# Attention and two expert layers: weight conversion through ScalarE's rectifier, and fixed steps for weight maxima and gating sums

## Chip, cores and metric

One core of one Trainium2 chip runs the whole program. The metric is the device time of one execution in microseconds (us). A difference of 0.2% (about 4 us) is what a measurement of this kernel can tell from no change.

## What is computed

Three stages follow each other. Inputs are float32 except the three weight matrices of the second stage, which come as float64 (a float32 array times a float64 scalar).

```python
def _attn_ref(q, k, v, tau):                 # 4 x 8 heads, 576 x 64
    scores = scale * np.matmul(q, k.transpose(0, 1, 3, 2))
    thresh = np.max(scores, axis=-1, keepdims=True) - tau
    scores = np.where(scores >= thresh, scores, -1000000000.0)
    attn = softmax(scores)
    return np.matmul(attn, v)

def _moe_ref(x, w_gate, w_val, w_out, rms_g):    # 2304 tokens, 512 -> 1536 -> 512
    xn = x / rms * rms_g
    g = xn @ w_gate
    silu = g * (1.0 / (1.0 + np.exp(-g)))
    return (silu * (xn @ w_val)) @ w_out

def _moe2_ref(x, w_gate, w1, w2):            # 8 experts, 512 -> 1024 -> 512
    P = np.exp(x @ w_gate - max)
    for _ in range(8):
        P /= P.sum(1, keepdims=True) + 1e-09
        P /= P.sum(0, keepdims=True) + 1e-09
        P *= N / E
    for e in range(E):
        out += P[:, e:e + 1] * (np.maximum(x @ w1[e], 0.0) @ w2[e])
    return out
```

## The kernel before

Every float32 operand of a matmul is split into two float16 parts, and a product takes three matmuls.

**Attention** (`att_tile`, from line 283). A tile is 128 rows of one head. TensorE computes the scores `S` (line 294, two PSUM buffers), VectorE takes their maximum (308), ScalarE the exponential (312), VectorE keeps what is within `tau` of the maximum (314), ScalarE and GpSimd split the result into `hl` (319 to 321), SyncE transposes it by DMA into `eT`, and four tiles later TensorE multiplies with the values (351). Eight tiles, one for each head, make 128 tokens `x`; `finish_x` (from line 363) normalises them (VectorE's last operation is line 374) and SyncE transposes them into `xnT`.

**Second stage.** Two such blocks make 256 tokens, for which `mlp_in` (from line 544) multiplies with the gate and value weights (`gv`, line 551, twelve pairs of PSUM tiles) and `mlp_out` (from line 573) with the output weights (585). Before the first of these the float64 weights must be converted. `prep_group` takes the gate weights (`wgate`) and value weights (`wval`) in 24 loads of 128 rows of 512 numbers; `prep_out` takes the output weights (`wo`) in 12. Each load is two 32-bit words for a number, read by `words` (434; four buffers for the 24 loads, two for the 12), and `to_f32` (445) makes float32 of it: the high word, read as a float32 and scaled by 2^-112, has the right bits but for a shift by three; ScalarE scales it (453), VectorE takes three bits from the low word (454), shifts and joins (456), and puts the sign bit back from the high word (457). ScalarE then squares the result for the scale (477 or 511), and each load is scaled and split: ScalarE 486 and VectorE 487 for gate and value; VectorE 528, ScalarE 529 and GpSimd 530 for the output weights. The first `mlp_in` needs gate and value weights, the first `mlp_out` the output weights. A planner sets the order of the instructions on each engine from priorities; attention has the higher one, and weight pieces fill in where it expects an engine to be free.

**Third stage** (its loop from line 1177). Its order on TensorE is written by hand. `ahead` is a list of steps `k`; a step is six matmuls of the first product (`X` or `Z`, line 1051), and after it come one or two pieces of six matmuls of the second product (`P`, line 1119). Fourteen steps make a round: three blocks of 128 pairs of tokens with seven pieces each, 21 pieces. The second products use three PSUM banks; the piece `j == 1` alone opens the bank with the tag `mx`, and VectorE empties it (1129 or 1133). Besides the logits at the stage's start, the same bank serves two things: the maximum of a half expert's weights over the partitions (`all_max`, 136, through `over_partitions`: TensorE 131, VectorE 133), and in the gating the maximum of the logits (`lgtop`) and the eight column sums (`cs`, line 1000, read by VectorE 1002). So a `P` of piece 1 that follows one of these waits until VectorE has read it, and one of these that follows a `P` of piece 1 waits until VectorE has emptied that.

The preparation of a half expert's weights (`weight`, from 787) is a generator of 17 pieces, and `AT` (831) lists the steps, counted from a base, at which they are issued; piece five is the maximum, pieces six to nine are GpSimd's four sums (823). For the first matrix of an expert the base is a multiple of 14, for the second it is 7 more.

```python
    AT = (0, 4, 6, 8, 10, 10, 11, 13, 15, 12, 14, 16, 17, 19, 21, 23, 24)
            for n in due.pop(k, ()):
                with behind():
                    next(n, None)
```

`sinkhorn` (974) is the gating: a generator, started at step 36 and advanced by one piece a step, six pieces an iteration, so that the column sums come at steps 43, 49, ... 85. Its result `lg` is needed by `coefs` (1014), by ScalarE's scaling of the accumulators (1158), and by VectorE's first accumulation with a coefficient (1129).

Of the kernel before, what the change touches and what calls it, by code (L numbers as in the profile page):

```python
# [7 lines left out]
F32 = mybir.dt.float32  # L8
# [3 lines left out]
AF = mybir.ActivationFunctionType  # L12
ALU = mybir.AluOpType
# [6 lines left out]
def kernel(  # L20
# [24 lines left out]
    V, A, G, T = nc.vector, nc.scalar, nc.gpsimd, nc.tensor  # L45
    B, H, S, D = q.shape
    NT, DM = out.shape
    DFF = moe_w_gate.shape[1]
    E, _, FF = moe2_w1.shape
# [11 lines left out]
    def small(shape, name, dt=F32, bufs=1):  # L61
        return p0.tile(shape, dt, tag=name, name=name, bufs=bufs)
# [65 lines left out]
    def over_partitions(col, eye, name):  # L128

        ps = psm.tile([P, P], F32, tag="mx", name=name + "p", bufs=1)  # L130
        T.matmul(ps, lhsT=col.to_broadcast([P, P]), rhs=eye, start=True, stop=True)
        m = small([P, 1], name, bufs=2)
        V.tensor_reduce(m, ps, AX.X, ALU.max)  # L133
        return m
# [310 lines left out]
    def to_f32(dst, word, name):  # L445

        lw = pw.tile([P, 2, 2, HD], F16, tag="xs", name=name, bufs=2)
        lw = lw.rearrange("p o l n -> p (o l n)").bitcast(I32)
        A.activation(dst, word[:, :, 1].bitcast(F32), AF.Copy, scale=2.0**-112)
        V.tensor_scalar(lw, word[:, :, 0], 29, None, ALU.logical_shift_right)
        di = dst.bitcast(I32)
        V.scalar_tensor_tensor(lw, di, 3, lw, ALU.logical_shift_left, ALU.bitwise_or)
        V.scalar_tensor_tensor(
            di, word[:, :, 1], -(2**31), lw, ALU.bitwise_and, ALU.bitwise_or
        )
        return lw  # L460

    staged = [0]
# [297 lines left out]
    @contextmanager  # L760
    def behind():

        with ExitStack() as es:
            for ins in main.values():
                es.enter_context(tc.issue_after(ins.ins))
            yield
# [61 lines left out]
            yield  # L828
        (w1, w2)[which - 1][h], (inv1, inv2)[which - 1][h] = w, inv

    AT = (0, 4, 6, 8, 10, 10, 11, 13, 15, 12, 14, 16, 17, 19, 21, 23, 24)

    w1, w2, inv1, inv2 = {}, {}, {}, {}

    def w_pool(h):
        return pb if h % 2 == 0 else pc
# [137 lines left out]
    def sinkhorn():  # L974

        V.scalar_tensor_tensor(
            lg, lg, ginv[:, 0:1], inv_tok.to_broadcast([P, NTL, E]), ALU.mult, ALU.mult
        )
        mx = small([P, 1], "lgm")
        V.tensor_reduce(mx, lg, AX.XY, ALU.max)  # L980
        yield
        yield
        top = over_partitions(mx, eye, "lgtop")
        V.tensor_scalar(top, top, -1.0, None, ALU.mult)
        A.activation(lg, lg, AF.Exp, bias=top[:, 0:1])
        yield
        for it in range(8):
            rsum = small([P, NTL], "skr", bufs=2)
            V.tensor_reduce(rsum, lg, AX.X, ALU.add)
            V.tensor_scalar(rsum, rsum, 1e-9, None, ALU.add)  # L990
            V.reciprocal(rsum, rsum)
            yield
            V.tensor_tensor(lg, lg, rsum.to_broadcast([P, NTL, E]), ALU.mult)
            yield
            csum = small([P, E], "skc", bufs=2)
            V.tensor_reduce(csum, lg.rearrange("p t e -> p e t"), AX.X, ALU.add)
            yield
            yield
            cps = psm.tile([P, E], F32, tag="mx", name=f"cs{it}", bufs=1)
            T.matmul(cps, lhsT=ones, rhs=csum, start=True, stop=True)  # L1000
            cinv = small([P, E], "ski", bufs=2)
            V.tensor_scalar(cinv, cps, 1e-9, None, ALU.add)
            V.reciprocal(cinv, cinv)
            V.tensor_scalar(cinv, cinv, float(NT // E), None, ALU.mult)
            yield
            V.tensor_tensor(
                lg,
                lg,
                cinv.rearrange("p (o e) -> p o e", o=1).to_broadcast([P, NTL, E]),
                ALU.mult,  # L1010
            )
            yield

    def coefs(h):
        c = small([P, NTL], "coef", bufs=3)
# [151 lines left out]
    steps = None  # L1167
    due = {}
    for hn in range(1, NE):
        for which, base in ((1, 42 * (hn - 1) + 14 * (hn == 1)), (2, 42 * (hn - 1) + 21 + 13 * (hn == 1))):  # L1170
            n = weight(which, hn, (lambda p: lambda: p)(w_pool(hn)))
            for x in AT:
                due.setdefault(base + x, []).append(n)
    owed = []
    gated = -1
# [1 line left out]
    with tc.manual_schedule(engines={mybir.EngineType.PE}):  # L1177
        for k, (c, j) in enumerate(ahead):
# [18 lines left out]
                owed = []  # L1197
            if h == 0 and f == 0 and j == 6 and g == NGR - 1:
                steps = sinkhorn()
                next(steps)  # L1200
                started = k
            elif steps is not None:
                with behind():
                    if next(steps, 0) == 0:
                        steps = None
            for n in due.pop(k, ()):
                with behind():
                    next(n, None)
# [3 lines left out]
            while done < min(want, len(later)):  # L1212
# [4 lines left out]
                if j == 0:  # L1217
                    m = u * NJ + jj + 2
                    if m == 2 * NGR * NJ:
                        while steps is not None:  # L1220
                            if next(steps, 0) == 0:
                                steps = None
# [42 lines left out]
```

## Time and profile before

| | |
|---|---|
| time, median of 3 runs | 2107.18 us (2106.46 to 2107.4) |
| the profiled execution | 2103.62 us, of which the profile's span 2101.7 us |
| TensorE (PE) busy | 1941.2 us, 92% |
| VectorE (DVE) busy | 1637.8 us, 78% |
| ScalarE (ACT) busy | 1306.4 us, 62% |
| GpSimd (POOL) busy | 1361.5 us, 65% |
| attention and second stage | 0 to 755 us |
| third stage | 755 us to the end |

The shares of the whole span say little here, because the stages have different limits: the slices of the page show TensorE at 1 to 4 tenths in the first 160 us and at 9 tenths or more after some 300 us, while VectorE stands at 6 to 9 tenths from the start.

### The profile page before, as it was taken

The page shows a single profiled execution, that of the slowest core. Times are in us where ns is not written, and L with a number is a line of the kernel's source. Part 1 is how long each engine was busy: PE and PEld are TensorE (multiplying, and loading weights), DVE is VectorE, ACT ScalarE, POOL GpSimd, SP SyncE. Part 2 cuts the span into 40 slices and gives each one's busy share as a digit, 9 for nine tenths or more (in the row PEclk, how much of TensorE's full clock was granted, in tenths as well). Part 3 has the DMA queues.
Part 4 walks back from the last instruction along what each step waited for, and adds up shares of the span by engine and source line. Part 5 has one row for each costly group of instructions (what it writes and reads, how often), then busy time and mean ns, then how long its engine had stood idle before and what let it go on. Part 6 is the DMA issues. An engine that isn't in the chain of part 4 may idle for free.

```text
span 2101.7 us, 43785 instructions
## 1 busy us (share of the span) xinstructions
PE 1941.2 (92%) x16462; PEld 1449.1 (69%) x16462; DVE 1637.8 (78%) x3408; ACT 1306.4 (62%) x2804; POOL 1361.5 (65%) x1412
## 2 busy tenths in 40 slices
PE   1448899999999999899999999999999999999998
PEld 0226577677877767677777777777777777777777
DVE  6998877778754536888888888888888888888865
ACT  6788778878753456557655555655555556555542
POOL 0436666657753566677767777777777677777754
PEclk9858999999999999999999999999999999999999
DMA  9976887977747645434433433443344334443332
GB/s 255 259 157 123 164 166 147 190 129 145 137 88 176 168 132 166 131 118 126 133 118 117 140 124 119 126 146 118 119 126 134 117 124 137 121 126 126 99 101 81
DMA packets 373093, 290.46 MB, mean 138 GB/s; under 512 B 286160, under 2 KB 299344, under 8 KB 372880
## 3 DMA queue, kind: packets, MB, share of 16 engines
q1 hardware_dynamic: 371712, 285.81, 52.2%
q8 instruction: 129, 2.11, 0.4%
q0 software_dynamic: 640, 1.84, 0.3%
q14 instruction: 84, 0.69, 0.1%
q10 hardware_dynamic: 528, 0.02, 0.0%
HBM read 195.71 MB, written 21.23 MB: 103 GB/s over the span
## 4 chain that ended last, share of the span: by engine, by line
PE 69%; DVE 2%; POOL 1%; issue 1%; ACT 0%; DMA 0%; DVEq 0%; POOLq 0%
PE P L1119 31%; PE X L1051 17%; PE Z L1051 13%; PE gv L551 4%; PE x L585 3%; DVE w L756 1%; PE pv L351 1%; PE S L294 0%; DVE acc L1133 0%; PE logits L900 0%; POOL w2s L823 0%; DMA eT<-hl 0%; POOL tT L566 0%; DVE w1mx L133 0%; DVE h L1030 0%
## 5 line engine op out<-in xcount | busy, mean ns | idle before, releaser
L1119 PE MATMUL P<-w,h 128*128 128x256 f16 x6048 | 767.5, 273 | 12.3 <-DVE w1mx L133 7.6
L1119 PEld LDWEIGHTS <-h 128*128 128x128 f16 x6048 | 591.3, 98 | 150.2 <-issue 15.3
L1051 PEld LDWEIGHTS <-w 128*128 128x128 f16 x4032 | 394.7, 98 | 193.8 <-issue 2.9
L1129 DVE SCALAR_TENSOR_TENSOR acc<-P,coef,acc 128x256 f32<-128x256 f32 x882 | 413.1, 478 | 99.7 <-PE P L1119 88.6
L1051 PE MATMUL X<-xo,w 128*128 128x384 f16 x2304 | 437.6, 326 | 1.3 <-ACT u2b L1071 0.9
L1051 PE MATMUL Z<-xo,w 128*128 128x384 f16 x1728 | 327.7, 326 | 0.0
L320 POOL TENSOR_TENSOR hl<-e,hl 128x512 f16<-128x512 f32 x144 | 172.6, 1199 | 216.3 <-ACT hl L319 135.3
L551 PE MATMUL gv<-xnT,wg 128*128 128x256 f16 x1296 | 166.7, 277 | 17.9 <-DVE u L561 12.9
L551 PE MATMUL gv<-xnT,wv 128*128 128x256 f16 x1296 | 165.2, 275 | 0.0
L551 PEld LDWEIGHTS <-wg 128*128 128x128 f16 x1296 | 126.0, 99 | 36.8 <-issue 19.5
L585 PE MATMUL x<-wo,tT 128*128 128x512 f16 x648 | 143.6, 379 | 0.8 <-DVE u L561 0.8
L551 PEld LDWEIGHTS <-wv 128*128 128x128 f16 x1296 | 127.0, 99 | 15.8
L314 DVE SCALAR_TENSOR_TENSOR e<-S,nt,e 128x576 f32<-128x576 f32 x144 | 116.3, 811 | 23.6 <-ACT e L312 22.9
L308 DVE TENSOR_REDUCE nt<-S 128x1 f32<-128x576 f32 x144 | 107.0, 750 | 29.5 <-PE S L294 28.9
L566 POOL TENSOR_TENSOR tT<-u,tT 128x256 f16<-128x256 f32 x108 | 78.4, 727 | 65.7 <-ACT tT L565 65.3
L312 ACT ACTIVATE e<-S,nt,c 128x576 f32<-128x576 f32 x144 | 117.3, 818 | 0.0
L585 PEld LDWEIGHTS <-tT 128*128 128x128 f16 x648 | 62.3, 98 | 72.3 <-ACT hl L319 1.0
L294 PE MATMUL S<-kT,qT 128*128 128x288 f16 (+1 forms) x320 | 65.5, 311 | 48.9 <-DVE e L314 41.1
L319 ACT ACTIVATE hl<-e 128x576 f16<-128x576 f32 x144 | 96.9, 677 | 18.8 <-DVE e L314 13.1
L351 PEld LDWEIGHTS <-eT 128*128 128x128 f16 (+1 forms) x2240 | 89.0, 105 | 25.1 <-DMA eT<-hl 10.5
L351 PE MATMUL pv<-vs,eT 128*128 128x64 f16 (+1 forms) x2240 | 96.8, 199 | 7.0 <-DMA eT<-hl 7.0
L294 PEld LDWEIGHTS <-qT 128*128 128x128 f16 (+1 forms) x320 | 23.6, 103 | 91.6 <-DVE e L314 54.3
(2540 smaller groups left out, 3710.5 us busy)
## 6 DMA issues: line engine op xcount, KB each, us to landing
xo<-x2s SPq DMA_DIRECT2D x319, 384.0 KB, 3.1
w1r<-in_moe_w_dram SPq DMA_DIRECT2D x17, 1024.0 KB, 5.1
w2r<-in_moe_w_dram SPq DMA_DIRECT2D x17, 1024.0 KB, 6.3
x2s<-xo SPq DMA_DIRECT2D x17, 384.0 KB, 2.7
wgatew<-in_moe_w_gate_dram SPq DMA_DIRECT2D x12, 512.0 KB, 5.7
wo<-in_moe_w_out_dram SPq DMA_DIRECT2D x12, 512.0 KB, 4.1
wvalw<-in_moe_w_val_dram SPq DMA_DIRECT2D x12, 512.0 KB, 4.1
qX<-qT SPq DMA_DIRECT2D x40, 128.0 KB, 2.6
```

Source lines behind the costliest of these rows:

```text
L294: last = T.matmul(sp[i * rows : (i + 1) * rows, j, 0:HS], lhsT=qq[:, h, 0:rows], rhs=kT[h // H2][:, h % H2, j * HS : (j + 1) * HS], start= ...
L308: V.tensor_reduce(mx, sv, AX.XY, ALU.max)
L312: A.activation(ev, sv, AF.Exp, bias=nt[:, 0:1], scale=st["c2"][:, c : c + 1])
L314: V.scalar_tensor_tensor(ev, sv, nt[:, 1:2], ev, ALU.is_ge, ALU.mult, accum_out=sums[:, slot : slot + 1])
L319: A.activation(hl[:, 0:S], e, AF.Copy)
L320: G.tensor_tensor(hl[:, S + REM :], e[:, 0 : NCH * P], hl[:, 0 : NCH * P], ALU.subtract)
L351: T.matmul(o, lhsT=a, rhs=r, start=n == 0, stop=n == len(mm) - 1)
L551: T.matmul(gv[:, a, :], lhsT=w[:, l, kk, f * P : (f + 1) * P], rhs=xt[:, r * KD + kk, :], start=n == 0, stop=n == 3 * KD - 1,)
L585: T.matmul(ps, lhsT=tT[f][:, l, o : o + P], rhs=wo[:, f, r, :], start=n == 0, stop=n == 3 * KF - 1,)
L1051: T.matmul(ps, lhsT=w[:, a, l, kk, f * P : (f + 1) * P], rhs=xb[:, r * 2 + kk, :], start=n == 0 and j in (0, 1, 3), stop=n == 5, skip_grou ...
L1119: T.matmul(ps, lhsT=hs[u, ao, f][:, l, jj * P : (jj + 1) * P], rhs=w2[h][:, bo, r, f, :], start=n == 0 and j in (0, 1, 3), stop=n == 5, sk ...
L1129: main[True] = V.scalar_tensor_tensor(y, ps, coef[h][:, i : i + 1], y, ALU.mult, ALU.add)
```

## The change

**In `to_f32`** ScalarE's Copy becomes Prelu with a slope of 2^32 for negative numbers, still scaled by 2^-112. A negative number comes out 2^32 times as large, so its exponent has bit 5 set, and VectorE's shift by three moves that bit to the place of the sign. Line 457, which put the sign back, goes; line 456 writes `wo` (or what stands for it) in place of `lw`.

**In `AT`** the first matrix of an expert has a list of its own: the maximum is issued one step later (11 in place of 10), GpSimd's first three sums at 11, 12 and 12 in place of 10, 11 and 12. The second matrix keeps its steps.

**In `sinkhorn`** a yield may name the steps of a round at which the generator goes on: the maximum of the logits at step 11 of a round, the column sums at steps 2 and 8. Other pieces are merged, so an iteration has three pieces and takes seven steps on average. The column sums come at steps 44, 50, 58, 64, 72, 78, 86 and 92. The last scaling of `cinv` is folded into the first operation.

```diff
-        A.activation(dst, word[:, :, 1].bitcast(F32), AF.Copy, scale=2.0**-112)
+        A.activation(dst, word[:, :, 1].bitcast(F32), AF.Prelu, scale=2.0**-112, alpha=2.0**32)
         V.tensor_scalar(lw, word[:, :, 0], 29, None, ALU.logical_shift_right)
         di = dst.bitcast(I32)
-        V.scalar_tensor_tensor(lw, di, 3, lw, ALU.logical_shift_left, ALU.bitwise_or)
-        V.scalar_tensor_tensor(
-            di, word[:, :, 1], -(2**31), lw, ALU.bitwise_and, ALU.bitwise_or
-        )
+        V.scalar_tensor_tensor(di, di, 3, lw, ALU.logical_shift_left, ALU.bitwise_or)
...
-    AT = (0, 4, 6, 8, 10, 10, 11, 13, 15, 12, 14, 16, 17, 19, 21, 23, 24)
+    AT = {
+        1: (0, 4, 6, 8, 11, 11, 12, 12, 13, 14, 15, 16, 17, 19, 21, 23, 24),
+        2: (0, 4, 6, 8, 10, 10, 11, 12, 13, 14, 15, 16, 17, 19, 21, 23, 24),
+    }
...
         V.tensor_reduce(mx, lg, AX.XY, ALU.max)
-        yield
-        yield
+        yield 11,
         top = over_partitions(mx, eye, "lgtop")
...
             V.tensor_tensor(lg, lg, rsum.to_broadcast([P, NTL, E]), ALU.mult)
-            yield
             csum = small([P, E], "skc", bufs=2)
             V.tensor_reduce(csum, lg.rearrange("p t e -> p e t"), AX.X, ALU.add)
-            yield
-            yield
+            yield 2, 8
             cps = psm.tile([P, E], F32, tag="mx", name=f"cs{it}", bufs=1)
             T.matmul(cps, lhsT=ones, rhs=csum, start=True, stop=True)
             cinv = small([P, E], "ski", bufs=2)
-            V.tensor_scalar(cinv, cps, 1e-9, None, ALU.add)
+            V.tensor_scalar(cinv, cps, 1e-9, E / NT, ALU.add, ALU.mult)
             V.reciprocal(cinv, cinv)
-            V.tensor_scalar(cinv, cinv, float(NT // E), None, ALU.mult)
             yield
...
-            yield
...
-            for x in AT:
+            for x in AT[which]:
                 due.setdefault(base + x, []).append(n)
...
                 steps = sinkhorn()
-                next(steps)
-                started = k
-            elif steps is not None:
+                places = next(steps)
+            elif steps is not None and (places is None or k % 14 in places):
                 with behind():
-                    if next(steps, 0) == 0:
-                        steps = None
+                    places = next(steps, 0)
+                if places == 0:
+                    steps = None
```

The order of instructions moves with it. Line numbers of the changed kernel are 3 lower after line 457 and 5 lower from the second half of `sinkhorn` on: its 525 is 528 here, its 1046 and 1114 are 1051 and 1119.

First VectorE, ahead of the last operation on the second block of tokens (`xn_866`, the one that the first `mlp_in` waits for). `wol` are the low words of the output weights, `wof` the scaled output weights, `nt` and `e` attention tiles. Before:

```order
245 L454 TENSOR_SCALAR wol_1663<-wo_1661 128x512
246 L487 SCALAR_TENSOR_TENSOR wv<-wo,wvalgs_1232,wv 128x512 x2
247 L456 SCALAR_TENSOR_TENSOR wol_1655<-wo,wol_1655 128x512
248 L369 TENSOR_SCALAR ms_868<-ssq_865 128x1
249 L456 SCALAR_TENSOR_TENSOR wol_1663<-wo,wol_1663 128x512
250 L457 SCALAR_TENSOR_TENSOR wo<-wo_1653,wol_1655 128x512
251 L314 SCALAR_TENSOR_TENSOR e_2_3_852,sums_2_723<-S_2_3_828,nt_2_3_849,e_2_3_852 128x576
252 L372 TENSOR_SCALAR rs_870<-rs_870,v_i 128x1
253 L457 SCALAR_TENSOR_TENSOR wo<-wo_1661,wol_1663 128x512
254 L314 SCALAR_TENSOR_TENSOR e_2_4_1909,sums_2_723<-S_2_4_1884,nt_2_4_1906,e_2_4_1909 128x576
255 L308 TENSOR_REDUCE nt_2_5_1946<-S_2_5_1925 128x1
256 L374 SCALAR_TENSOR_TENSOR xn_866<-x_863,rs_870,xn_866 128x512
```

With the change, in the same place:

```order
241 L308 TENSOR_REDUCE nt_2_4_1870<-S_2_4_1848 128x1
242 L525 TENSOR_SCALAR wof<-wo,wosf 128x512 x2
243 L314 SCALAR_TENSOR_TENSOR e_2_3_852,sums_2_723<-S_2_3_828,nt_2_3_849,e_2_3_852 128x576
244 L369 TENSOR_SCALAR ms_868<-ssq_865 128x1
245 L314 SCALAR_TENSOR_TENSOR e_2_4_1873,sums_2_723<-S_2_4_1848,nt_2_4_1870,e_2_4_1873 128x576
246 L525 TENSOR_SCALAR wof<-wo,wosf 128x512
247 L308 TENSOR_REDUCE nt_2_5_1910<-S_2_5_1889 128x1
248 L372 TENSOR_SCALAR rs_870<-rs_870,v_i 128x1
249 L525 TENSOR_SCALAR wof<-wo,wosf 128x512
250 L308 TENSOR_REDUCE nt_2_6_1945<-S_2_6_1924 128x1
251 L374 SCALAR_TENSOR_TENSOR xn_866<-x_863,rs_870,xn_866 128x512
```

Before, 30 of the 36 loads are converted ahead of this operation and six behind it; with the change all 36, and the first four of line 528, stand ahead of it, with 23 attention tiles begun in place of 22. The twenty-fourth load, the last of gate and value, stood behind 14 attention tiles and now stands behind 8.

Then TensorE at one weight maximum of the third stage (`w1mxp`). `P_0_1` is a piece 1, which opens the shared bank; `P_1_0` opens another. Before:

```order
20188 L1051 LDWEIGHTS w_6_17060
20189 L1051 MATMUL Z_3_18035<-xo_2_17564,w_6_17060 128x384
20190 L131 LDWEIGHTS w1m
20191 L131 MATMUL w1mxp<-ident,w1m 128x128
20192 L1119 LDWEIGHTS h_1_0_17582
20193 L1119 MATMUL P_0_1_18060<-w_5_16513,h_1_0_17582 128x256
```

With the change:

```order
20224 L1046 LDWEIGHTS w_6_17016
20225 L1046 MATMUL X_17874<-xo_5_17570,w_6_17016 128x384
20226 L131 LDWEIGHTS w1m
20227 L131 MATMUL w1mxp<-ident,w1m 128x128
20228 L1114 LDWEIGHTS h_0_0_17378
20229 L1114 MATMUL P_1_0_18052<-w_5_16469,h_0_0_17378 128x256
```

The maximum stood directly ahead of piece 1 of the shared bank; it now stands 12 matmuls behind the six of that piece, and the next matmul needs another bank.

## Rows read from the trace of the kernel before

**Rows 1.** Busy us by stretch: PE, PEld, DVE, ACT, POOL; clock; DMA share; GB/s
```profile
20.00:110.00 90.00, 33.57 (x218) 17.48 (x218) 85.84 (x189) 72.37 (x142) 23.79 (x25) 0.90 0.96 255
110.00:155.00 45.00, 17.74 (x166) 12.36 (x165) 43.75 (x91) 35.61 (x78) 16.91 (x19) 0.58 0.72 149
155.00:218.00 63.00, 51.42 (x545) 41.47 (x544) 55.96 (x139) 53.65 (x132) 38.09 (x46) 0.88 0.64 126
...
300.00:600.00 300.00, 287.92 (x3216) 217.90 (x3215) 233.66 (x548) 241.66 (x562) 197.12 (x266) 1.00 0.78 146
...
755.00:870.00 115.00, 106.00 (x912) 76.46 (x911) 76.36 (x148) 78.49 (x180) 85.36 (x82) 0.99 0.55 158
870.00:1000.00 130.00, 127.71 (x982) 95.83 (x981) 110.09 (x242) 79.89 (x163) 92.64 (x86) 1.00 0.42 130
1000.00:2090.00 1090.00, 1084.84 (x8334) 814.59 (x8332) 887.33 (x1720) 614.67 (x1272) 786.50 (x729) 1.00 0.39 121
```

**Rows 2.** Line 457 alone, by stretch: length, VectorE busy us (count); their sum
```profile
20.00:110.00 90.00, 16.35 (x21) 0.90 0.96 255
...
sum 198.00, DVE 27.16; mean DVE 9.05
```

**Rows 3.** Timeline of VectorE, 51.9 to 55 us: start us, us, operation
```profile
51.96 0.69 DVE L457 SCALAR_TENSOR_TENSOR wo<-wgatew,wgatel 128x512 int32<-128x512 int32 x1
52.56 0.81 DVE L314 SCALAR_TENSOR_TENSOR e<-S,nt,e 128x576 f32<-128x576 f32 x1
...
54.62 0.42 DVE L454 TENSOR_SCALAR wgatel<-wgatew 128x512 int32<-128x512 int32 x1
```

**Rows 4.** Line 528 on VectorE: duration ns min/median/max, first and last start us
```profile
L528 DVE TENSOR_SCALAR wof<-wo,wosf x12: 471/503/1366, 190.2 to 228.0; 128x512 f32<-128x512 f32 x12
```

**Rows 5.** Line 453 on ScalarE: duration ns min/median/max, first and last start us
```profile
L453 ACT ACTIVATE wo<-wvalw x12: 642/650/675, 29.5 to 109.3; 128x512 f32<-128x512 f32 x12
L453 ACT ACTIVATE wo<-wo x12: 647/661/677, 110.2 to 171.2; 128x512 f32<-128x512 f32 x12
```

**Rows 6.** Groups of ScalarE by line, 20 to 180 us: busy us, mean ns
```profile
L486 ACT ACTIVATE wg<-wo,wgategs 128x512 f16<-128x512 f32 x12 | 7.7, 709 | 0.0
```

**Rows 7.** Timeline of ScalarE, its first instruction
```profile
9.59 1.28 ACT L181 ACT_TABLE_LOAD   x1 [9.59 <-DMA raw_k<-in_k_dram]
```

**Rows 8.** Waits of SyncE, 20 to 180 us: total us, times, longest
```profile
SPq L442 <- DVE wo L457: 17.8, 10, 5.6
```

**Rows 9.** Timeline of TensorE, first gating tile and first output tile
```profile
155.25 2.72 PE L551 MATMUL gv<-xnT,wg 128*128 128x256 f16 x12 [4.30 <-DMA xnT<-xn]
...
218.09 4.91 PE L585 MATMUL x<-wo,tT 128*128 128x512 f16 x22 [0.77 <-DVE u L561]
```

**Rows 10.** Waits of TensorE, 155 to 220 us
```profile
PE gv L551 <- DVE u L561: 8.3, 2, 5.5
```

**Rows 11.** Waits of TensorE, 755 us to the end
```profile
PE P L1119 <- DVE w1mx L133: 7.6, 14, 2.6
PE P L1119 <- DVE ski L1002: 3.3, 1, 3.3
PE cs L1000 <- DVE acc L1133: 1.6, 1, 1.6
PE P L1119 <- DVE lgtop L133: 0.8, 1, 0.8
```

**Rows 12.** Timeline of TensorE at one weight maximum
```profile
1101.45 0.22 PE L131 MATMUL w1mxp<-ident,w1m 128*128 128x128 bf16 x1
1102.05 1.14 PE L1119 MATMUL P<-w,h 128*128 128x256 f16 x9 [0.38 <-DVE w1mx L133]
```

**Rows 13.** Timelines of VectorE, ScalarE, VectorE where the gating ends
```profile
923.20 0.70 DVE L1017 TENSOR_TENSOR coef<-coef,inv_tok 128x18 f32<-128x18 f32 x2
...
942.05 1.32 ACT L1158 ACTIVATE acc<-acc,coef 128x512 f32<-128x512 f32 x2
...
957.75 0.47 DVE L1129 SCALAR_TENSOR_TENSOR acc<-P,coef,acc 128x256 f32<-128x256 f32 x1
```

## Prediction

> **What bounds the kernel now.** I read the busy times by stretch first [rows 1], and in them who is full in each. From 20 to 110 us VectorE is busy 85.84 of 90 us and from 110 to 155 us 43.75 of 45, while TensorE has 33.57 and 17.74 and ScalarE 72.37 and 35.61: the conversion of the float64 weights and the first attention tiles go at VectorE's pace. The DMA share of 0.96 in the first of these is the other number to keep in mind. From 300 us on TensorE is busy 287.92 of 300, and after 1000 us 1084.84 of 1090: whatever comes earlier into these stretches ends earlier. Between, from 755 to 870 us, TensorE idles 9.0 us, and 2.3 from 870 to 1000.
>
> Then the places. The first gating matmul of the second stage starts at 155.25 us, after a wait for `xnT`, and the first output matmul at 218.09 [rows 9]; in these 62.8 us TensorE waits 8.3 us for VectorE's line 561 [rows 10]. In the third stage the waits of TensorE [rows 11] name the shared bank four times: 7.6 us for the read of a weight maximum (14 times), 3.3 for that of a column sum, 1.6 for a bank not yet emptied before a column sum, 0.8 for the logits' maximum, 13.3 us together. Rows 12 are one case [rows 12]: the maximum's matmul at 1101.45, and the next `P` only at 1102.05, 0.38 us of it idle.
>
> **Part one, the conversion.** Line 457 goes: 36 operations, 27.16 us busy, 16.35 of it before 110 us [rows 2]. An operation starts 0.09 us before the one ahead of it ends (51.96 to 52.56 for one of 0.69, [rows 3]), so on VectorE's own path it is 27.16 - 36 x 0.09 = 24 us, 0.60 us each where nothing stretches it. Line 456 keeps its shape and only writes elsewhere: nothing. The buffer of a load comes free one operation earlier, and SyncE waits for line 457 ten times, 17.8 us in all, to issue the next load [rows 8].
>
> Prelu in place of Copy: no row shows one. Copy of this shape takes 650 to 661 ns [rows 5], and with one more operand from memory 709 [rows 6]; I take the same as Copy, at the worst 36 x 0.05 = 1.8 us of ScalarE, which has 27 us idle between 20 and 155 us. It cannot come out below nothing, since a pass over the same elements stays.
>
> How much of the 24 us arrives? The planner does not simply close the gaps. Ahead of the second block's last VectorE operation (the one that the first gating matmul waits for) it removes 30 of the 36, 30 x 0.60 = 18.0 us, but moves ahead six loads' lines 454 and 456, 6 x (0.42 - 0.09 + 0.60) = 5.6 us [rows 3], four of line 528, 4 x 0.41 = 1.7 [rows 4], one tile's maximum and eleven short ones, some 2 us. So 18.0 - 9.3 = 8.7: the first gating matmul comes 9 us earlier, at 146, if VectorE stays the pace. ScalarE gets six loads more ahead of it, some 8 us, out of its 27 idle ones.
>
> What was moved ahead is missing afterwards: of VectorE's 55.96 us in the stretch 155 to 218 some 13 go (six loads at 0.33 + 0.60 + 0.60, four of line 528, the short ones), and ScalarE loses about as much of 53.65 [rows 1]. Of TensorE's 11.6 idle us there I take 5 back. Sum of part one: 9 + 5 = **14 us**. Its upper bound is all of VectorE's 24. Its lower one: if DMA sets the pace up to 110 us, its share of 0.96 leaves 90 - 86 = 3.6 us there; I put 3. I take 14 because the rows of VectorE are full in both stretches and those of DMA only in one. VectorE's next limit is ScalarE: without line 457 it has about 71 us of work up to 110, ScalarE 72.
>
> **Part two, the shared bank.** `w1mxp` moves from directly ahead of piece 1 to 12 matmuls behind it, and the next user of the bank is further off than the maximum's read takes. The second matrix's maximum, which stands in that place already, has no row with a `P` waiting for it. So the 7.6 us go; the column sums, now at two such places a round, give back 3.3 + 1.6, and the logits' maximum 0.8. I take **12** of 13.3, since VectorE is full there (110.09 of 130 us, [rows 1]) and its backlog may be waited for elsewhere. Bounds: 14 x 0.38 = 5 (only the regular waits) and 13.3. What is moved costs nothing where I look: GpSimd's three sums come a step later, but the fourth stays and ScalarE's first split follows where it did. The dropped scaling of `cinv` is VectorE's time, not TensorE's.
>
> The gating ends seven steps later (column sum at step 92 for 85). A step is 1345 us / 672 = 2.0 us, so 14 us. `coefs` ended at 923.9, ScalarE's scaling began at 942.05 and VectorE first used the result at 957.75 [rows 13]: 18 us of slack cover 14, and another 15 lie behind them.
>
> **Sum.** 14 + 12 = 26 us: the profiled execution's 2103.62 (span 2101.7) would be 2077.6. The median of the runs, 2107.18, is 3.6 above it; from it **2081 us**.
>
> A rule speaks against the change. Of the tables of ScalarE the trace shows one load in the whole program, 1.28 us, before its first operation [rows 7], and the changed order has one too. The Trainium skill (ScalarE activation tables: per-element evaluation and per-set limits, "What a function is on this engine") says that two functions of different sets are one table load apart, at 1283 ns; the row agrees on the size, and no row here shows a switch. Were Prelu in another set than the exponential, each of 36 would bring up to two loads: 36 x 2 x 1.28 = 92 us on ScalarE, of which its 27 idle and the 26 gained would hide half; 2150 us. That is a rival with a chance of 1%.
>
> **Rivals.**
> 1. *All of it arrives* (12%): 24 + 13.3 = 37 us, 2070. For it: TensorE's idle time before 300 us is far more than 24. Against it: ScalarE and DMA are nearly as full.
> 2. *DMA takes over the early pace* (18%): share 0.96 up to 110 us, and the new order wants the same 24 loads behind 8 tiles instead of 14. Part one gives 4, the sum 16: 2091. Against it: waits of SyncE for line 457 show that loads could be issued earlier.
> 3. *The waits return elsewhere* (8%): VectorE's backlog in the gating is waited for by another bank. Part two gives nothing, the sum 14: 2093.
> 4. *No change within 0.2%* (4%): 2 and 3 together, 4 us: 2103.
> 5. *Slower: attention starves behind the weights* (7%). All 36 loads now stand ahead of the second block's end. The last twelve go through two buffers, and took (171.2 - 110.2) / 11 = 5.5 us each [rows 5]. If that is their own turnaround and not VectorE's queue, and the first 24 still end at 109.3, six more loads put the first gating matmul 6 x 5.5 = 33 us later, at 188. The next stretch gives 11.6 back at most, part two 12: 2107 + 33 - 11.6 - 12 = 2117. It decides from about 183 us on: 28 us late is what the rest pays for, 4 us more show. For it: ten waits of SyncE are only 17.8 us, so most of the 5.5 is not that wait. Against it: VectorE's queue in those 61 us was full, and each load passed it three times.
>
> The forecast, with between a half and all of both parts, has 50%.
>
> **How the numbers follow.** Low end: 2107 - 24 - 13.3 = 2069.9, and 1 for the stretched operations: 2069. High end: 3 + 5 = 8 off, 2099, and 1 for the spread: 2100. That holds the forecast and rivals 1 to 3, 88%, less some for their edges. Faster by over 0.2% (4.2 us, about what a measurement can tell): 50 + 12 + 18 + 8 = 88%; within: 4%; slower: 7 + 1 = 8%.
>
> **What would show it.** Right: the first gating matmul near 146 us and the first output matmul near 204; ScalarE's line 453 for the 24th load well before 109; VectorE no longer at 95% up to 110 us; no `P` waiting for `w1mx`, `ski` or `lgtop`; TensorE idle under 3 us between 755 and 1000 for 11.3 now; the stretch after 1000 us shorter by the 12 regular waits, 4.6 us. Wrong in part one: VectorE or ScalarE waiting for the weights' DMA, or the first gating matmul at 155 or later. Wrong in part two: idle time of TensorE of the same size, put down to lines 1129 or 1133, or ScalarE's line 1158 late. Prelu above 709 ns, or a second table load, would tell on the rectifier.

## The result, and the profile after

The changed kernel takes **2080.38 us** (median of 4 runs, 2076.74 to 2084.12) against 2107.29 (2106.46 to 2108.33) before, a ratio of 0.9872 with a 95% interval of 0.9857 to 0.9888. Two later comparisons gave 0.9887 [0.9871, 0.9904] and 0.9864 [0.9846, 0.9883]. The forecast was 2081. Executions of the kernel before lay between 2099.9 and 2113.2 us over all comparisons, so times are compared within one of them, and places in the program from trace to trace. The profiled execution of the changed kernel took 2080.2 us, its span is 2078.4: 23.3 us less than before.

The stretches answer to [rows 1] (columns as there):

```profile
20.00:110.00 90.00, 32.41 (x203) 16.58 (x203) 85.72 (x203) 82.15 (x164) 21.55 (x23) 0.72 1.00 276
110.00:155.00 45.00, 25.35 (x255) 18.11 (x255) 36.18 (x81) 39.04 (x90) 28.69 (x33) 0.68 0.86 174
155.00:218.00 63.00, 57.61 (x647) 43.60 (x645) 52.13 (x125) 52.90 (x125) 37.39 (x49) 0.97 0.75 126
218.00:300.00 82.00, 73.19 (x777) 53.48 (x776) 58.12 (x146) 63.64 (x147) 50.99 (x70) 1.00 0.88 168
300.00:600.00 300.00, 286.98 (x3272) 219.50 (x3271) 229.29 (x540) 237.98 (x551) 192.68 (x265) 1.00 0.77 143
755.00:870.00 115.00, 107.02 (x899) 79.65 (x898) 81.68 (x157) 73.36 (x168) 81.44 (x76) 0.99 0.57 157
870.00:1000.00 130.00, 127.80 (x982) 95.68 (x980) 116.29 (x238) 83.13 (x169) 91.15 (x85) 1.00 0.38 119
```

Up to 110 us VectorE is as full as before (85.72 us of 90), ScalarE has gone from 72.37 to 82.15 and DMA from 255 to 276 GB/s: in the same time more weights are converted. What went is seen one stretch later, where VectorE falls from 43.75 of 45 us to 36.18, and TensorE gains 7.6 us from 110 to 155 and 6.2 from 155 to 218. From 755 to 870 TensorE has 107.02 for 106.00: hardly anything, though most of the waits of [rows 11] were to go there, and from 870 to 1000 it is where it was (127.80 for 127.71). The same rows show something else: TensorE's granted clock, as a share of the upper of its two levels (2.4 GHz; the lower, 1.2 GHz, is 0.50), is 0.97 for 0.88 from 155 to 218 us and 1.00 for 0.98 from 218 to 300.

The rectifier itself, line 453 by its input (duration min/median/max in ns, first and last start), answers to [rows 5]:

```profile
L453 ACT ACTIVATE wo<-wgatew x12: 640/652/666, 20.6 to 69.8; 128x512 f32<-128x512 f32 x12
L453 ACT ACTIVATE wo<-wvalw x12: 642/660/684, 28.9 to 84.0; 128x512 f32<-128x512 f32 x12
L453 ACT ACTIVATE wo<-wo x12: 643/662/677, 86.1 to 126.9; 128x512 f32<-128x512 f32 x12
```

Its 652 to 662 ns are Copy's. The 24th load is converted at 84.0 us instead of 109.3, and the twelve loads of the output weights take (126.9 - 86.1) / 11 = 3.7 us each, not 5.5. ScalarE's timeline has one table load, at its start, as in [rows 7]:

```profile
9.48 1.28 ACT L181 ACT_TABLE_LOAD   x1 [9.48 <-DMA raw_k<-in_k_dram]
```

The first gating and the first output matmul, in the timeline of TensorE, answer to [rows 9]:

```profile
147.75 2.72 PE L548 MATMUL gv<-xnT,wg 128*128 128x256 f16 x12 [0.64 <-DMA xnT<-xn]
...
204.44 5.78 PE L582 MATMUL x<-wo,tT 128*128 128x512 f16 x26
```

They come 7.5 and 13.7 us earlier. TensorE's waits from 720 to 1010 us and from there to the end answer to [rows 11]:

```profile
PE w1mxp L131 <- DVE acc L1128: 5.2, 2, 4.0
PE P L1114 <- DVE acc L1128: 2.0, 4, 0.8
PE Z L1046 <- DMA xo<-x2d: 1.5, 1, 1.5
...
PE P L1114 <- DVE ski L999: 0.3, 1, 0.3
```
```profile
PE P L1114 <- DVE acc L1124: 0.6, 1, 0.6
```

The twelve regular waits after 1000 us are gone, and `lgtop`, `w1mx` and `cs` stand in no row; but a wait that was not there before, 4.04 us long, stands ahead of `w1mxp`. The timelines of TensorE and VectorE around it:

```profile
826.79 1.14 PE L1046 MATMUL X<-xo,w 128*128 128x384 f16 x6
831.97 0.27 PE L131 MATMUL w1mxp<-ident,w1m 128*128 128x128 bf16 x1 [4.04 <-DVE acc L1128]
```
```profile
825.35 1.41 DVE L753 SCALAR_TENSOR_TENSOR w<-w2r,w_s,w 128x512 f16<-128x512 f32 x1
826.68 0.95 DVE L793 TENSOR_TENSOR w1m<-w1m 128x1 f32<-128x1 f32 x1
827.56 1.56 DVE L753 SCALAR_TENSOR_TENSOR w<-w2r,w_s,w 128x512 f16<-128x512 f32 x1
829.04 0.19 DVE L1000 RECIPROCAL ski<-ski 128x8 f32<-128x8 f32 x1
829.15 0.37 DVE L1128 TENSOR_TENSOR acc<-P,acc 128x256 f32<-128x256 f32 x1
829.44 0.61 DVE L1002 TENSOR_TENSOR lg<-lg,ski 128x144 f32<-128x144 f32 x1
829.98 1.39 DVE L753 SCALAR_TENSOR_TENSOR w<-w2r,w_s,w 128x512 f16<-128x512 f32 x1
831.29 0.29 DVE L988 TENSOR_REDUCE skr<-lg 128x18 f32<-128x144 f32 x1
831.50 0.41 DVE L1128 TENSOR_TENSOR acc<-P,acc 128x256 f32<-128x256 f32 x1
```

TensorE is ready at 827.9 and must have the bank `mx`, which the piece before it filled. The operation that empties it (line 1128, 831.50) stands in VectorE's queue behind two splits of the second half expert's `w2` (line 753: scaled weights, less their float16 part) and a round of the gating (lines 1000, 1002, 988). At the end of this wait the granted clock falls to the lower level, from 831.8 to 835.2 us (columns as in [rows 1]):

```profile
831.80:835.20 3.40, 3.23 (x13) 1.88 (x13) 1.88 (x7) 0.79 (x2) 0.00 (x0) 0.50 0.71 243
```

VectorE waits for the weights' DMA, too, which the prediction gave as a sign against part one. From 20 to 130 us:

```profile
DVE wol L454 <- DMA wo<-in_moe_w_out_dram: 5.2, 3, 3.5
```

The longest of these three waits, 3.51 us, ends at 125.29, ahead of the first gating matmul (two more traces of this kernel have 5.4 and 4.3 us in all).

By places: the first `P` of the third stage comes at 759.15 us for 775.88, so 16.7 us are gained up to it, and from there to the end the program takes 1319.3 us for 1325.8, 6.5 less. In three traces of the changed kernel the first gating matmul comes at 146.75 to 148.06 us, the first output matmul at 202.4 to 204.5, the first `P` at 756.8 to 760.3, and the rest takes 1317.7 to 1319.3: differences of one or two us between two traces say nothing.

### The profile page after: what moved, and what is told of

It is laid out like the page before. It is cut to its first block, busy times and chain, and to the rows that moved or that the text cites. A ratio compares the mean times of both kernels' runs of the same rounds, so it can differ in the third digit from the quotient of the medians.

```text
span 2078.4 us, 43779 instructions
## 1 busy us (share of the span) xinstructions
PE 1937.0 (93%) x16462; PEld 1444.5 (70%) x16462; DVE 1612.3 (78%) x3364; ACT 1299.5 (63%) x2804; POOL 1348.8 (65%) x1412
## 4 chain that ended last, share of the span: by engine, by line
PE 67%; DVE 3%; POOL 1%; issue 1%; DMA 1%; ACT 1%; SPq 0%; DVEq 0%; POOLq 0%; ACTq 0%
PE P L1114 30%; PE X L1046 16%; PE Z L1046 12%; PE gv L548 4%; PE x L582 3%; DVE w L753 1%; DMA xo<-x2d 1%; PE pv L351 0%; DVE acc L1128 0%; PE S L294 0%; DVE h L1025 0%; SPq L858 0%; PE logits L900 0%; POOL tT L563 0%; DVE lg L992 0%
## 5 line engine op out<-in xcount | busy, mean ns | idle before, releaser
L1114 PEld LDWEIGHTS <-h 128*128 128x128 f16 x6048 | 590.8, 98 | 145.6 <-issue 10.1
L582 PE MATMUL x<-wo,tT 128*128 128x512 f16 x648 | 143.2, 379 | 0.6 <-DVE u L558 0.6
L351 PEld LDWEIGHTS <-eT 128*128 128x128 f16 (+1 forms) x2240 | 86.1, 104 | 37.2 <-DMA eT<-hl 24.3
L753 DVE SCALAR_TENSOR_TENSOR w<-w1r,w_s,w 128x512 f16<-128x512 f32 x64 | 84.2, 1331 | 7.0 <-ACT w L752 7.0
```

Source lines behind the costliest of these rows:

```text
L351: T.matmul(o, lhsT=a, rhs=r, start=n == 0, stop=n == len(mm) - 1)
L582: T.matmul(ps, lhsT=tT[f][:, l, o : o + P], rhs=wo[:, f, r, :], start=n == 0, stop=n == 3 * KF - 1,)
L753: V.scalar_tensor_tensor(dst[1], src, s, dst[0], ALU.mult, ALU.subtract)
L1114: T.matmul(ps, lhsT=hs[u, ao, f][:, l, jj * P : (jj + 1) * P], rhs=w2[h][:, bo, r, f, :], start=n == 0 and j in (0, 1, 3), stop=n == 5, sk ...
```

## The experiments

In the comparisons below "third stage" is the time from the first `P` to the end of the span.

**One part alone: the conversion.** The kernel before with the two pieces of `to_f32` changed, as in the diff above, and nothing else.

> The conversion alone, the shared bank as in the kernel before. Theory: it is worth what the changed kernel's trace shows up to the first P, 16.8 us, and nothing after it: 2107.3 - 17 = 2090, first gating matmul of the second stage near 147.8 us, first output matmul near 204.4, first P near 759, the stretch from there to the end 1326 us as before. Rival one (the prediction's sum): 14 us, 2093, the 3 us between the first output matmul and the third stage not its own. Rival two (it also shortens the gating, since VectorE comes to it with less behind): 20 us or more, 2087 or below.

Measured: 2087.29 us against 2102.78, ratio 0.9927 [0.9914, 0.9941], so 15.5 us. First gating matmul at 148.1 us, first output matmul 204.8, first `P` 758.9, all as in the changed kernel; third stage 1328.4, 2.6 more than before, of which 2.0 are TensorE's busy time (1307.72 for 1305.75; the granted clock is at its lower level from 829.0 to 832.4 and from 852.9 to 856.3, before only from 866.7 to 870.1). So the whole gain ahead of the third stage is the conversion's, and none of it lies behind. The theory's 17 and the prediction's 14 lie both in the interval (12 to 18 us).

**One part alone: the bank.** `AT` and `sinkhorn` changed, `to_f32` as before.

> The shared bank's part alone (maxima and column sums at fixed steps), the conversion as before. Theory: 6.5 us as in the changed kernel's trace after the first P: 4.6 from the regular waits and 2 in the gating, because VectorE's queue there takes 4 us back: 2107.3 - 6.5 = 2100.8, and one wait of 3 to 5 us of TensorE for VectorE's line 1133 ahead of w1mxp in the gating. Rival (the prediction's sum): 12 us, 2095, no TensorE wait over 1 us in the gating; the 4 us of the changed kernel would then come from the two parts together. First gating matmul of the second stage stays at 155.3 us in either.

Measured: 2093.16 against 2102.78, ratio 0.9956 [0.9942, 0.9970], 9.6 us (6 to 12), so the times alone decide neither for 6.5 nor for 12. Third stage 1318.4, so 7.4 less than before. TensorE's waits, 720 to 1010 us:

```profile
PE w1mxp L131 <- DVE acc L1131: 5.2, 2, 4.0
PE P L1117 <- DVE acc L1131: 2.7, 4, 1.1
```

The new wait is there to the hundredth (4.04 us, in this kernel at 844.86) without the conversion: it belongs to the bank's part.

**The changed kernel again**, beside these two.

> The changed kernel once more, beside its two parts on the same chip. The median is expected at 2080 (2077 to 2084). If the parts add up, it stands at 2107.3 less both gains: theory 17 + 6.5 = 23.5, so 2084; prediction 14 + 12 = 26, so 2081. More than 2 us below the sum of the two gains measured means that they help each other.

Measured: 2079.38 against 2102.78, 23.4 us, while the two parts alone gave 15.5 + 9.6 = 25.1. Within the intervals they add up; that one helps the other is not seen.

**The maxima alone.** Of the bank's part only `AT`.

> The kernel before with the weights' table of steps alone; the gating's column sums keep their old steps, the conversion is as before. Theory: the 12 regular waits for w1mx after 1000 us (4.6 us) go and nothing else that is regular; the column sums' waits (ski 3.3, cs 1.6, lgtop 0.8) stay, and the gating's maximum waits in VectorE's queue as before. So 4.6 to 7 us from before, against 9.6 for the whole of the bank's part, and the third stage from its first P 4 to 6 us shorter than 1325.8. Rival: the whole gain of the bank's part, 8 us or more, is the maxima's.

Measured: 2100.54 against 2107.8, ratio 0.9967 [0.9953, 0.9980], 7.3 us; third stage 1320.9, 4.9 less. No regular wait after 1000 us is left, `ski` 3.3, `cs` 1.6 and now `lgtop` 1.6 stay, and `w1mxp` waits 2.3 for the emptying of the bank. By the third stages (4.9 of 7.4 us) the maxima bring two thirds of the bank's part, as the theory had it; the times (2.8 to 9.9 us) don't exclude the rival's 8.

**Less in VectorE's queue, first try.** `w2` of the second half expert six steps earlier.

```diff
-21 + 13 * (hn == 1)
+21 + 7 * (hn == 1)
```

> The changed kernel with the second expert half's w2 six steps earlier (base 28 instead of 34), so that its splits no longer stand between the next maxima and their matmul in VectorE's queue during the gating. Theory: the 4.04 us that TensorE waits ahead of w1mxp in the gating are VectorE's backlog, and fall below 1 us; the time falls by 3 to 4 us against the changed kernel, to about 2077. Rival one: VectorE has no room for them earlier either, a wait of the same size appears a few us before (lgtop, first column sum), and the time stays at 2080. Rival two: the wait is for something else than VectorE's queue and stays where it is.

Measured: 2076.25 beside 2079.38 for the changed kernel (ratios to before 0.9876 [0.9858, 0.9894] and 0.9887 [0.9871, 0.9904]: the intervals overlap); the wait is still 3.30 us. Three of the seven splits, those of the sums, had only taken the place of the others: the expectation of under 1 us failed though the time came near the 2077 expected, and this run can't tell the theory from its first rival.

**Less in the queue, second try.** Both matrices of that half expert earlier, so that all seven splits are done before the place.

```diff
-((1, 42 * (hn - 1) + 14 * (hn == 1)), (2, 42 * (hn - 1) + 21 + 13 * (hn == 1)))
+((1, 42 * (hn - 1) + 7 * (hn == 1)), (2, 42 * (hn - 1) + 21))
```

> The changed kernel with both matrices of the second expert half earlier (w1 at step 7 instead of 14, w2 at 21 instead of 34), so that none of their seven w2 splits lies in VectorE's queue after step 44. With the splits only six steps earlier the wait ahead of w1mxp went from 4.04 to 3.30 us, while three splits of 0.74 to 1.57 us still stood ahead of the bank's eviction there. Theory (VectorE has more work than time between the gating's start and that matmul, and every us taken out of it comes off the wait): the three splits are worth 3.6 us, the wait falls under 1 us, the time is 3 to 4 us below the changed kernel, 2076. Rival: the wait is the eviction's own place behind the gating's chain of short operations, not the amount of work; it stays at 3 us or more and the time at 2078 to 2080.

Measured: 2075.89 us against 2105.03, ratio 0.9863 [0.9846, 0.9879]. The timelines of TensorE and VectorE at the same place:

```profile
826.02 0.22 PE L131 MATMUL w1mxp<-ident,w1m 128*128 128x128 bf16 x1
```
```profile
820.99 0.15 DVE L793 TENSOR_TENSOR w1m<-w1m 128x1 f32<-128x1 f32 x1
...
824.63 0.42 DVE L1128 TENSOR_TENSOR acc<-P,acc 128x256 f32<-128x256 f32 x1
```

`w1mxp` waits for nothing there. Third stage 1312.0 us, 7.3 less than in the changed kernel and 13.8 less than before. TensorE's idle time in it is 9.3 us for 14.9 in the changed kernel and 20.1 before, so of the 7.3 us idle time makes 5.6. The rest is the granted clock: the fall at 831.8, right behind the long wait, is absent (no stretch at the lower level in the third stage up to the last `P`), and it had cost some 1.6 us (an estimate: twelve gating matmuls take 2.72 us at the lower level, at 147.75 in the changed kernel, and 1.47 at the upper, at 162.17, so 46% of 3.4 us). That 13.8 is near the 13.3 of [rows 11] is in part chance: other waits stay, and the clock adds to it. The rival, that the eviction stands behind the gating's chain and not behind the work, falls.

**The same steps in the kernel before.** Does the backlog cost anything there?

> The kernel before with only the steps of the second expert half's weights moved (w1 at 7, w2 at 21), both of the change's parts left out. Theory: VectorE's queue in the gating is as full in the kernel before, so the waits that name it there (w1mx 2.6, ski 3.3, w1m 0.8, cs 1.6) shrink by 2 to 5 us and the 12 regular waits of 4.6 us stay: 2100 to 2103 against 2105. Rival: the backlog matters only with the change's order of the maxima; no difference within 1 us in the third stage, 1325 to 1327 us from its first P.

Measured: 2109.0 against 2107.8, ratio 1.0006 [0.9994, 1.0019], and the third stage 1331.6, 5.8 longer than before. The theory fell. In the timeline of TensorE:

```profile
847.13 0.22 PE L131 MATMUL w1mxp<-ident,w1m 128*128 128x128 bf16 x1
850.38 1.47 PE L1119 MATMUL P<-w,h 128*128 128x256 f16 x12 [3.02 <-DVE w1mx L133]
```

With the old table the read of the maximum is issued right behind a round of the gating, and this `P` waits 3.02 us for it with no split in VectorE's queue, where it waited 2.60 before; and the splits now meet the gating's start, where `lgtopp` waits 1.46 us and a `P` 1.58 for its result. Of the 5.8 us TensorE's idle time makes 2.8 (22.8 for 20.1). Most of the rest is the clock again: it is at the lower level from 814.6 to 821.4, from the middle of these waits at the gating's start on, and from 872.7 to 876.1, 10.2 us for 3.4 before, some 3 us by the same estimate. There the order was the reason, and moving the work didn't help; only once the order is changed does the amount of work decide. The two have to go together.

**Both versions side by side.**

> The changed kernel again, beside the version with both matrices of the second expert half earlier, on one chip: 2079 to 2080, third stage 1318 to 1319 us from its first P, with the wait of 4.04 us ahead of w1mxp.

> The version with both matrices of the second expert half earlier, again. Theory: 4 us of VectorE's backlog and about 3 us of smaller waits behind it are gone, so the third stage is 1312 us from its first P and the time 4 to 6 us below the changed kernel of the same call. Rival: the difference of the two medians so far (2075.9 to 2079.4, from two chips) was chance, and they come out within 2 us.

Measured: 2079.13 (2074.42 to 2081.42) and 2075.60 (2073.85 to 2076.94), ratios to before 0.9864 [0.9846, 0.9883] and 0.9851 [0.9833, 0.9869]. Third stages 1319.3 and 1311.8, the wait of 4.04 us in the one and not in the other, twice now each. In the two profiled executions the new version is 4.9 us ahead (2076.50 to 2081.42): 7.5 in the third stage, less 2.6 by which its first `P` came later (762.9 for 760.3). Both third stages without the wait lack the fall of the clock behind it. The gain in the third stage is settled. The times differ by 3.5 us, between the theory's 4 to 6 and the rival's 2, and their intervals still overlap.

**What paces the conversion now.** Three kernels, each meant to have less of one resource ahead of the first gating matmul. The first leaves out the low words:

```diff
-        V.tensor_scalar(lw, word[:, :, 0], 29, None, ALU.logical_shift_right)
         di = dst.bitcast(I32)
-        V.scalar_tensor_tensor(di, di, 3, lw, ALU.logical_shift_left, ALU.bitwise_or)
+        V.tensor_scalar(di, di, 3, None, ALU.logical_shift_left)
```

> The changed kernel without the low word: the pass that shifts it right by 29 is left out, and the join becomes a shift alone, so the weights lose their three lowest bits. It takes 36 x (0.42 - 0.09) = 12 us off VectorE's own path ahead of the second stage's first gating matmul and leaves DMA and ScalarE as they are. If VectorE still sets the pace of the conversion: that matmul comes 8 us or more earlier than 147.75, at 140 or below. If DMA has taken over (share 1.00 of its time from 20 to 110 us in the changed kernel): less than 3 us earlier, 145 or later, and the time within 3 us of 2080.

The second reads every second load only (`if kk % 2 == 0` and `if f % 2 == 0` ahead of `words`):

> The changed kernel with every second load of float64 weights left out and the one before it converted twice in its place: half the weights are then copies. The 18 loads of 0.52 MB would take 1.9 us each at the 276 GB/s that DMA moved from 20 to 110 us; the engines' work is as before. If DMA sets the pace: the first gating matmul of the second stage 5 us or more earlier than 147.75, up to where VectorE (85.7 of 90 us busy) or ScalarE (82.2) is full, so 138 to 143. If VectorE or ScalarE sets it: 146 or later.

The third squares only the first of four loads (`if kk == 0`):

> The changed kernel with three of four of ScalarE's squares of the gate and value weights left out (18 passes of 0.65 us; the norms are then made of one square taken four times): 11.7 us less of ScalarE before 84 us, DMA and VectorE as they are. If ScalarE has become the pace: the first gating matmul 6 us or more earlier than 147.75. If DMA or VectorE: less than 3 us.

Measured, in the same order, the first gating matmul: 137.68, 148.13 and 146.78 us, for 147.75. The first of them:

```profile
137.68 2.35 PE L547 MATMUL gv<-xnT,wg 128*128 128x256 f16 x12 [0.25 <-DMA xnT<-xn]
```

The stretch from 20 to 110 us (TensorE, its weight loads, VectorE, ScalarE, GpSimd; clock; DMA share; GB/s), one kernel after the other:

```profile
20.00:110.00 90.00, 36.48 (x225) 16.97 (x224) 73.18 (x183) 84.74 (x172) 21.69 (x27) 0.75 1.01 276
```
```profile
20.00:110.00 90.00, 32.57 (x185) 15.17 (x184) 85.44 (x199) 81.16 (x163) 20.27 (x20) 1.00 0.75 189
```
```profile
20.00:110.00 90.00, 31.81 (x207) 16.79 (x206) 86.64 (x205) 73.12 (x145) 20.07 (x22) 0.72 0.99 273
```

Half the loads away, DMA falls to 0.75 and 189 GB/s, and the first gating matmul doesn't move; 9 us less of ScalarE leave it within the spread of three traces; less of VectorE brings 10.1 us. So VectorE sets the pace of the changed kernel up to this matmul, and there a DMA share of 1.00 was no bound.

None of the three takes away one resource alone. The kernel without low words lost more of VectorE than the 12 us of its expectation: the join, now a shift alone, takes 426 ns in the median for some 690, and the planner put one load and the four operations of line 528 behind. VectorE is busy 90.0 us of the 133.3 ahead of `xn_866`, for 116.5 of 143.2: 26.4 us went and 10 arrived. VectorE then waits for TensorE's scores and for ScalarE, which has 84.74 of 90 us, the most of these kernels: that fits the next limit that the prediction named, but was not tried. VectorE's longest waits from 20 to 143 us:

```profile
DVE nt L308 <- PE S L294: 9.1, 10, 2.2
DVE wo L455 <- ACT wo L453: 7.2, 11, 2.1
```

With half the loads VectorE's waits for the output weights' DMA are gone, and the planner puts six operations of line 528 ahead for four; the first output matmul comes 5.5 us earlier (198.89), outside the spread. So behind the first gating matmul the loads may cost time in the changed kernel; this run can't tell that from the planner's other order. With fewer squares none of the operations of line 528 stands ahead.

One thing was not expected. Without the low words the first output matmul comes 7.2 us earlier than in the changed kernel (197.25), but the first `X` of the third stage only 1.0 (685.05 for 686.08), and the one execution took 2077.27 us; with half the loads the first `X` is not earlier either (687.58). TensorE's waits, 200 to 690 us, of the changed kernel and of the one without low words:

```profile
PE pv L351 <- DMA eT<-hl: 11.3, 15, 2.9
...
PE gv L548 <- DVE u L558: 2.5, 2, 1.3
```
```profile
PE pv L351 <- DMA eT<-hl: 14.6, 18, 2.8
PE gv L547 <- DVE u L557: 6.3, 2, 4.3
```

The waits for transposed attention tiles and for the gating function grow, but others shrink: from the first output matmul to the first `P`, which takes 560.8 us for 554.7, TensorE's idle time is 26.5 for 24.1 us, 2.4 of the 6.1. The rest is busy time (534.4 for 530.6): the granted clock, in the changed kernel at the upper level throughout this part, is at the lower one from 340.9 to 344.3 and from 525.2 to 532.0. The second fall comes in the longest wait:

```profile
518.43 1.47 PE L547 MATMUL gv<-xnT,wg 128*128 128x256 f16 x12
...
526.95 2.72 PE L547 MATMUL gv<-xnT,wg 128*128 128x256 f16 x12 [4.34 <-DVE u L557]
```

Whether the planner's other order or the attention's own pace causes the waits was not tried.

## Why the prediction was right, step by step

**The conversion: 14 us forecast, 15.5 measured alone.** The counting behind it held. The first output matmul came 13.7 us earlier, against 14, in two pieces: 7.5 where 9 stood ("the first gating matmul comes 9 us earlier, at 146, if VectorE stays the pace"), and 6.2 where 5 stood. The condition is now shown: VectorE stayed the pace. That removing 24 us from its path would bring only a third there, since loads move ahead into the room, is in the trace: all 36 loads start by 126.9 us.

What the sum left out is 3 us more between the first output matmul and the third stage. From 218 to 300 us, where VectorE has 6 us less now (58.12 for 64.47), TensorE's idle time went from 11.4 us to 8.8; before it was:

```profile
218.00:300.00 82.00, 70.59 (x776) 53.31 (x777) 64.47 (x141) 64.65 (x147) 52.47 (x68) 0.98 0.91 176
```

But the same times hold other work now, 13.7 us further on in the program. From the first output matmul to the first `P` it took 557.8 us and takes 554.7, and TensorE's idle time gives only 1.2 of the 3.1 (25.3 to 24.1); its busy time gives 1.9, most of it from the clock, which before was at the lower level from 248.9 to 252.3 us (some 1.6 by the estimate above). Two other traces of the changed kernel have one such fall there, too, and take 554.4 and 555.8. The prediction has no term for the clock. The premise that "whatever comes earlier into these stretches ends earlier" held for this change and failed for the kernels without low words and with half the loads, so it is no rule.

Two of the signs were wrong. VectorE was to be "no longer at 95% up to 110 us": it is at 95% still, with more loads done, and the sign that fits is the next stretch. And VectorE's wait for the weights' DMA, a sign that part one is wrong, came (5.2 us) while part one held.

**Prelu at Copy's cost** was right (652 to 662 ns), and so was the one table load. The Trainium skill (ScalarE activation tables: per-element evaluation and per-set limits, "What a function is on this engine") counts a table load where two functions lie in different sets; the trace has none after the first, so here that price was not paid.

**The bank: 12 us forecast, 9.6 measured alone (6.3 to 12.2), 6.5 and 7.4 in the traces' third stages.** Here a step was mis-sized. The regular waits went as forecast (4.6 us). All the gating's waits of [rows 11] went too, except 0.3 of `ski`. But in their place came 4.04 us ahead of `w1mxp`, 1.2 at another maximum and 2.0 for emptied banks. The prediction took 1.3 us off for "its backlog may be waited for elsewhere"; by the traces it was 6 to 7. The sign set for it failed: TensorE idles 10.2 us between 755 and 1000, for 11.3 before, where under 3 was forecast. That is rival 3's mechanism in part. VectorE is busy 15.4 of the 16.4 us from 815.6 to 832.0:

```profile
815.60:832.00 16.40, 12.05 (x93) 8.85 (x92) 15.38 (x24) 8.79 (x20) 12.95 (x12) 0.99 0.32 96
```

The averages of [rows 1], 76.36 of 115 us and 110.09 of 130, on which the 1.3 rested, don't show that. With the work moved out of these 16 us the third stage was 7.3 us shorter than in the changed kernel.

**The slack of `coefs`** held. The gating's last column sum comes at 912.66 for 918.18, so 11 us later counted from the first `P`, and ScalarE's first scaling, at 924.45, comes 165.3 us after the first `P`, where it came after 166.2 ([rows 13]).

**The rivals.** *All of it arrives*: no, 28.7 of 37 us at most. *DMA takes over*: not up to the first gating matmul, by the half loads; behind it that stays open. *The waits return elsewhere*: in part, as said. *No change*: no, all three intervals end below 0.991. *Slower, attention starves behind the weights*: the first gating matmul at 147.75 and 3.7 us a load for the output weights, so at most 3.7 of the 5.5 before were the loads' own turnaround. (Its working has a slip: by its own terms the rest pays for 11.6 + 12, some 24 us, not 28; 28 is with the 4 that show.) *Table loads*: none.

The sum, 26, lies among the 26.9, 23.4 and 28.7 us of the three comparisons. By the traces it is 23.3: 2.7 too little ahead of the third stage and 5.5 too much in it, which partly cancel. That the forecast met the time so closely is therefore more than its steps deserve.

## What to carry to other kernels

An engine that is full in a stretch still gives up time when work is taken from it, but what is moved ahead into the room must be counted against it: here a third of 24 us came at the first place that waited, and 9 more up to the third stage. A share of 1.00 of DMA is no bound until a kernel with fewer loads says so, and then place by place: with half the loads the first gating matmul stayed and the first output matmul came earlier. Compare traces from one place of the program to another, not between the same times, and split what differs into TensorE's idle time and its granted clock: a long wait cost more than its own length where the clock fell behind it. Where a shared buffer's reader is moved away from a busy place, look at the queue of the engine that empties it over the few us in front, not over the stage's average; and try a lighter queue together with the new order: here it cost 6 us of the third stage with the old one and gave 7 with the new.

## What the runs showed of the hardware

An operation on one column of VectorE (line 793, the maximum of two numbers a partition) took 151 ns in the median and 954 at the place of the wait:

```profile
L793 DVE TENSOR_TENSOR w1m<-w1m x14: 146/151/954, 826.7 to 1903.4; 128x1 f32<-128x1 f32 x14
```
```profile
826.17 1.45 POOL L1084 TENSOR_TENSOR u6c<-u6a,u6c 128x384 f32<-128x384 f32 x1
```

GpSimd's line 1084 ran from 826.17 to 827.62, VectorE's operation from 826.68 to 827.63: they end together. The kernel before has the same: 951 ns from 840.85, beside GpSimd's line 1087, both ending at 841.8. In either kernel the 27 other operations of this line, none beside one of GpSimd, took 156 ns at most. In the version with both matrices earlier the same operation, at 820.99, began just before GpSimd's next one (821.08) and took 0.15 us, and the largest of its 14 was 152 ns. The Trainium skill (SBUF — State Buffer, "Who interferes with whom") says that a VectorE instruction with two SBUF inputs contends with a GpSimd instruction that reads SBUF; these rows agree. They point to GpSimd for part of VectorE's backlog: the splits at the wait took 1.39 to 1.56 us, while in the other version one at 807.42, with GpSimd idle until 808.14, took 0.74, and one at 810.68, beside GpSimd's line 1084, took 1.04. How much of the 4 us that makes was not tried.
